# Top-32 attention and mixture of experts on one core: the threshold's selection moves from VectorE to GpSimd, and the pipeline gets a step longer

## Chip, cores and metric

One core of one Trainium2 chip runs the whole program. The metric is the device time of one execution in microseconds, the median of several runs.

## What is computed

Attention over 8 batches of 8 heads, 576 positions and 64 dimensions, in which each row keeps only its 32 largest scores. Its output, 4608 rows of 512, goes through a mixture of 8 experts, of which each row uses one.

```python
scores = scale * np.matmul(q, k.transpose(0, 1, 3, 2))
kth = np.partition(scores, -top_k, axis=-1)[..., -top_k:-top_k + 1]
scores = np.where(scores >= kth, scores, -1000000000.0)
attn = np.exp(scores - np.max(scores, axis=-1, keepdims=True))
attn = attn / (np.sum(attn, axis=-1, keepdims=True) + 1e-09)
x = np.matmul(attn, v)                        # -> rows of 512
logits = x @ w_gate + modality_bias[modality_id]
e_idx = np.argmax(logits, axis=1)
h = np.maximum(x[mask] @ w1[e], 0.0)          # mask: the rows of expert e
out[mask] = gate_w[mask, None] * (h @ w2[e])
```

## The kernel before

The scores are made in 288 tiles of 128 rows by 576, nine for each pair of heads, four pairs for each of the 8 batches. The main loop has one step `i` for each tile, and in a step each engine works on tiles of different age. In step `i`:

- TensorE makes the scores of tile `i + 2` (`qk`) and transposes the weights of tile `i - TL` (`trans`). It also makes parts of attention times v (`av`), transposes of later k and q (`prep`), transposes of finished rows (`xrow`, one row block of `x` each) and pieces of expert work.
- ScalarE copies scores out (`sevac`), makes a sign mask `K` (`sign`), which says which scores lie below the 24th largest and whose sum `n` tells how many do, exponentials (`expo`), and copies for TensorE.
- VectorE takes the 8 largest of seven parts of tile `i` (`subs`, L337), merges those of tile `i - 1` to its 24 largest (`chain`, L348 to L350), and takes the next 8 below them from the product `y` of an older tile (`find`, L379). When `find` has been made for three tiles, `pick` (L386 to L388) chooses among the nine values from the 24th to the 32nd the one that is the threshold: `eq` compares `i9s` with `n`, `jk` multiplies by the values, and an add over nine gives `kth`. In the same step the masked product `keep` (L399) of the oldest of these three tiles follows: scores at or above `kth`, times the exponentials.
- GpSimd runs `gate` (L403, one element, which waits for the `keep` of the step before), `pool_y` (L375, the product `y` of scores and sign mask), `below` (L362) and `small` (L356), in that order, and in some steps `fill` (L302), copies of tokens, and the issue of indirect DMAs: scatters of rows of `x` (L534) and of finished output rows (L724), each with a memset (L460) behind it.

VectorE's instructions of a step are put in order by `weave`: `chain` between `subs`, with `find` at place 2 and the operations on rows of `x` that `xrow` has left (`late`) at the places in `LOP`. What stands in the list `c_` comes after these: small operations of routing and of the expert schedule, `pick`, and `keep` last. Each engine runs its instructions in the order in which they are written.

Expert work is cut into slots of 256 rows of one expert. While the loop runs, a planner adds pieces of a slot to TensorE's queue: in each step it gets the budget `STEP` less the estimated `COST` of the attention work. 12 slots are handled in this woven way, with the weights in full fp32 (L685, L697, L709). The slots that remain go through a tail of their own (`slot`, L1074 and L1090), in which weights and rows are split in two parts each (`parts`, L1029, L1030), and three products are made of them. The first tail slot needs its weights split and its rows transposed (`turn_rows`, L1045). 19 slots are worked on in all, 7 of them in the tail.

```python
LT = LY + 1
LR = LT + 2
LE = LR - 1
TL = LR + 2
```

`LT` is the age of the tile of `find`, `LR` that of `keep`, `LE` that of `expo`, and `TL` that of `trans`. `RX` lists the steps of a batch's 36 in which `xrow` is made; the step after each has the operation on VectorE. `PJ` lists the steps of nine in which the transposes of the next pair's last rows, k and q are made. `AV3` and `AV7` cut `av` in parts for successive steps.

Of the kernel before, what the change touches and what calls it, by code (L numbers as in the profile page):

```python
# [9 lines left out]
FT = mybir.dt.float32  # L10
# [4 lines left out]
OP = mybir.AluOpType  # L15
# [6 lines left out]
CAP = 2.6  # L22
ME = 23
NB = 4
# [4 lines left out]
NW = 3  # L29
STEP = 3.3  # L30
STEPS = {"small": 0.1, "late": 0.5, "more": 0.15}
LJ = (5, 6)
PJ = (0, 1, 3)
VJ = 7
# [3 lines left out]
LY = KL + 2  # L38
LT = LY + 1
LR = LT + 2  # L40
LE = LR - 1
TL = LR + 2
YB = 3
XB = 3
RL = (5, 6)
RX = (1, 3, 10, 12, 14)
HG = 2
CUT = (12, 26)
PB = (2, 4)
AV3 = (0, 3, 5)  # L50
AV7 = (0, 2, 5)
COST = {"trans": 0.5, "qk": 0.5, "mix": 1.12, "rest": 0.22, "t": 0.11, "prep": 0.43, "logits": 1.2, "xrow": 0.54, "av": 0.49, "av8": 0.17}
# [17 lines left out]
def kernel(  # L70
# [301 lines left out]
    def pool_y(i):  # L372
        t = T[i]
        t["y"] = wk.tile([128, S], FT, name="y", bufs=YB)
        G.tensor_tensor(t["y"], t["S"], t["K"], op=OP.mult)  # L375
# [5 lines left out]
    def pick(i):  # L381

        t = T[i]
        eq, v = (wk.tile([128, 3, 9], FT, name=nm, bufs=1) for nm in ("eq", "jk"))
        n = t["n"][:, 0, :]
        return [lambda: V.tensor_tensor(eq, i9s, n[:, :, None].to_broadcast([128, 3, 9]), op=OP.is_equal),  # L386
                lambda: V.tensor_tensor(v, eq, t["mg"][:, :, 23:32], op=OP.mult),
                lambda: V.tensor_reduce(kth[:, i - 2:i + 1], v, axis=AX.X, op=OP.add)]  # L388

# [11 lines left out]
    def gate(i):  # L401

        G.tensor_scalar(spare[:, 0:1], T[i]["P"][0:1, 0:1], 1.0, 1.0, op0=OP.mult, op1=OP.mult)  # L403
# [442 lines left out]
    for i in range(LAST):  # L846
# [39 lines left out]
        for f in lp:  # L886
            f()
        cost += COST["rest"] * (len(lp) > 0)
        if p + 1 < NPAIR and j in PREP:
            prep(p + 1, PREP[j])  # L890
            cost += COST["t" if PREP[j] == "t" else "prep"]
# [27 lines left out]
        u = i - (TL + 1)  # L919
        if avs:  # L920
            c, f = avs.popleft()
            f()
            cost += c
        if ok(u) and u % 9 in (3, 7, 8):
# [29 lines left out]
        if ok(i - LT):  # L954
            b_.insert(2, lambda: find(i - LT))
            if (i - LT) % 3 == 2:
                c_ += pick(i - LT)
        for x, f in enumerate(lo):
# [24 lines left out]

        if ok(i - 1 - LR):
            gate(i - 1 - LR)
        if ok(i - LY):
            pool_y(i - LY)
        if ok(i - 1):
# [263 lines left out]
```

## Time and profile before

| what | us |
|---|---|
| median of 3 runs (1341.92 to 1348.37) | 1348.02 |
| the profiled execution | 1345.19 |
| span of its profile | 1343.4 |
| TensorE (PE) busy, share of the span | 1227.5, 91% |
| VectorE (DVE) | 1174.4, 87% |
| ScalarE (ACT) | 1001.1, 75% |
| GpSimd (POOL) | 630.0, 47% |

The profile is of one execution. Its times count from the first instruction; the execution's own time is 1.8 us longer than the span. Busy time is what the instructions of an engine cover. Matmuls are pipelined, and their ends are modelled, so a full TensorE in the profile need not be a TensorE at its peak. In the rows further down PE, DVE, ACT, POOL and SP are TensorE, VectorE, ScalarE, GpSimd and SyncE, and L399 is line 399.

### The profile page before, as it was taken

How to read it: one execution, taken by the hardware profiler on the slowest of the kernel's cores; microseconds unless marked ns; L12 is line 12 of the kernel's file. 1: busy time of each engine (PE TensorE's matmuls, PEld its weight loads, DVE VectorE, ACT ScalarE, POOL GpSimd, SP SyncE). 2: the span in 40 equal slices, each digit the busy share in tenths (PEclk: the TensorE clock that was granted, in tenths of full speed). 3: DMA queues.
4: the chain of work that ended last, by engine and by line, in shares of the span. 5: the costliest groups of instructions: out<-in, count | busy, mean ns of one | idle time of the engine just before them, and what ended most of it. 6: DMA issues, size and time to landing. Idle time of an engine off the chain costs nothing. (4 is left out here: it accounts for less than half of the span.)

```text
span 1343.4 us, 28995 instructions
## 1 busy us (share of the span) xinstructions
PE 1227.5 (91%) x8101; PEld 927.1 (69%) x8101; DVE 1174.4 (87%) x5958; ACT 1001.1 (75%) x1997; POOL 630.0 (47%) x1250
## 2 busy tenths in 40 slices
PE   6788887799998999999789999999999998999996
PEld 4666666576775867686567676876777665689985
DVE  3999999999999999999999999999999952666762
ACT  3788877888888879898888878988898851545642
POOL 2455547445565547554744575557554722011110
PEclk7899999899999999999989999999999999999998
DMA  5565334575545755653477556746664325656640
GB/s 118 137 177 124 81 81 115 147 198 142 135 116 163 201 134 160 185 142 81 131 189 193 134 157 165 176 112 196 166 176 126 124 80 177 219 181 228 236 170 15
DMA packets 206787, 201.05 MB, mean 150 GB/s; under 512 B 106221, under 2 KB 153325, under 8 KB 206608
## 3 DMA queue, kind: packets, MB, share of 16 engines
q1 hardware_dynamic: 200400, 179.48, 50.3%
q0 software_dynamic: 6208, 19.54, 4.0%
q8 instruction: 69, 1.13, 0.4%
q14 instruction: 110, 0.90, 0.2%
HBM read 118.63 MB, written 24.23 MB: 106 GB/s over the span
## 5 line engine op out<-in xcount | busy, mean ns | idle before, releaser
L337 DVE MAX8 cand<-Ssb 128x8 f32<-128x82 f32 (+1 forms) x2016 | 415.9, 229 | 19.9 <-ACT Ssb L330 19.8
L375 POOL TENSOR_TENSOR y<-Ssb,K 128x576 f32<-128x576 f32 x288 | 367.2, 1275 | 3.1 <-ACT K L369 2.6
L324 PE MATMUL S<-ks,qs 128*128 128x288 f32 x1024 | 234.9, 352 | 61.4 <-ACT Ssb L330 44.6
L330 ACT ACTIVATE Ssb<-S 128x576 f32<-128x576 f32 x288 | 187.9, 653 | 109.8 <-PE S L324 75.5
L369 ACT ACTIVATE K<-Ssb,n 128x576 bf16<-128x576 f32 x288 | 226.3, 786 | 31.2 <-POOL y L375 30.8
L324 PEld LDWEIGHTS S<-ks,qs 128*128 128x128 f32 x1024 | 160.0, 194 | 118.2 <-ACT Ssb L330 64.9
L393 ACT ACTIVATE ex<-Ssb,sm 128x576 f32<-128x576 f32 x288 | 224.2, 779 | 0.0
L399 DVE SCALAR_TENSOR_TENSOR P<-Ssb,kth,ex 128x576 f32<-128x576 f32 x256 | 213.5, 834 | 10.7 <-ACT ex L393 0.5
L379 DVE MAX8 mg<-y 128x8 f32<-128x576 f32 x288 | 213.8, 742 | 2.5 <-POOL y L375 2.5
L697 PE MATMUL E<-xgT,w1b 128*128 128x256 f32 x768 | 191.0, 392 | 6.7 <-ACT hT L701 4.5
L422 ACT ACTIVATE PT<-T 128x640 f32<-128x640 f32 (+1 forms) x288 | 190.0, 660 | 7.4 <-PE T L414 7.3
L709 PE MATMUL E<-w2b,hT 128*128 128x512 f32 x384 | 184.9, 605 | 2.2 <-ACT ot L719 1.3
L414 PE MATMUL T<-idf,P 128*128 128x128 f32 x1152 | 172.5, 277 | 0.0
L697 PEld LDWEIGHTS E<-xgT,w1b 128*128 128x128 f32 x768 | 140.6, 192 | 39.3 <-ACT hT L701 8.1
L443 PE MATMUL X<-PT,vm 128*64 128x256 f32 (+1 forms) x1536 | 163.2, 341 | 3.0 <-ACT st L260 2.5
L362 POOL TENSOR_SCALAR n<-mg 128x1 f32<-128x1 f32 x288 | 69.2, 240 | 201.9 <-DVE mg L350 198.2
L403 POOL TENSOR_SCALAR spare<-P 1x1 f32<-1x1 f32 x256 | 47.8, 187 | 219.4 <-DVE mg L348 204.2
L414 PEld LDWEIGHTS T<-idf,P 128*128 128x128 f32 x1152 | 138.0, 142 | 2.8 <-ACT PT L422 0.9
L443 PEld LDWEIGHTS X<-PT,vm 128*64 128x64 f32 x1536 | 80.8, 138 | 56.6 <-issue 27.0
L709 PEld LDWEIGHTS E<-w2b,hT 128*128 128x128 f32 x384 | 66.0, 190 | 64.2 <-issue 57.3
L1096 POOL DMA_INDIRECT out_dram<-ot,tk x14 | 14.0, 1003 | 131.0 <-ACT ot L1095 131.0
L348 DVE MAX8 mg<-cand 128x8 f32<-128x56 f32 x288 | 61.5, 214 | 0.2
(208 smaller groups left out, 2213.8 us busy)
## 6 DMA issues: line engine op xcount, KB each, us to landing
w1b<-in_moe_w_dram SPq DMA_DIRECT2D x76, 512.0 KB, 4.6
w2b<-in_moe_w_dram SPq DMA_DIRECT2D x76, 512.0 KB, 5.6
ks<-st SPq DMA_DIRECT2D x64, 288.0 KB, 3.9
qs<-st SPq DMA_DIRECT2D x128, 144.0 KB, 4.1
ks<-st SPq DMA_DIRECT2D x62, 256.0 KB, 5.0
xg<-xs SPq DMA_DIRECT2D x19, 516.0 KB, 5.9
km<-in_k_dram SPq DMA_DIRECT2D x64, 128.0 KB, 5.0
qm<-in_q_dram SPq DMA_DIRECT2D x64, 128.0 KB, 2.9
```

Source lines behind the costliest of these rows:

```text
L324: PE.matmul(ps[:, hf, u - a:v - a], l, d["ks"][:, x, h, u + o:v + o], start=(n == 0), stop=(n == len(terms) - 1), skip_group_check=(j == 8))
L337: return [lambda s=s: V.max(c[:, s * 8:s * 8 + 8], T[i]["S"][:, bnd[s]:bnd[s + 1]]) for s in range(NSUB)]
L369: A.activation(t["K"], t["S"], AF.Sign, scale=2.0 ** -24 - 1.0, bias=t["n"][:, 1, i % 3:i % 3 + 1], accum_out=t["n"][:, 0, i % 3:i % 3 + 1])
L375: G.tensor_tensor(t["y"], t["S"], t["K"], op=OP.mult)
L379: V.max(t["mg"][:, i % 3, 24:32], t["y"])
L393: A.activation(t["ex"], t["S"], AF.Exp, bias=t["s"][:, i % 3:i % 3 + 1])
L399: V.scalar_tensor_tensor(t["P"], t["S"], kth[:, i:i + 1], t["ex"], op0=OP.is_ge, op1=OP.mult, accum_out=dn)
L414: PE.transpose(T[i]["pt"][:, x, :], (Pm if c == 4 else Pb[c % 2])[:, h * 512 + x * 128:h * 512 + x * 128 + 128], idf)
L422: A.activation(o, T[i]["pt"][:, :n], AF.Copy)
L443: PE.matmul(o.rearrange("p (a b) -> p a b", a=2) if j < 8 else o, l, r, start=(c == 0), stop=(c == 4))
L697: PE.matmul(ps[:, f % 2], w1b[:, c, f * 128:(f + 1) * 128], xgT[:, c, :], start=(c == 0), stop=(c == KC - 1))
L709: PE.matmul(o["py"], hT[:, f, t * 128:(t + 1) * 128], w2b[:, f, :], start=(f == 0), stop=(f == FC - 1))
```

## The change

`pick` no longer compares. GpSimd makes five small operations for it: the difference `d` of `i9s` and `n`, its square, the square cut off at 1 (0 where both are equal, 1 elsewhere), its product with the values, and the values less that product. What is left is the chosen value and eight zeros, and VectorE adds the nine. The call stands one step later than before, behind `gate` and `pool_y`, which are now written ahead of the step's `c_`. `LR` is `LT + 3`: `keep`, `expo` and `trans` work on tiles one step older, and there is one more buffer of scores and one less of `y`. The rest are numbers of the planner, the places of `xrow`, the steps of the k and q transposes, the cut of `av`, and the place in the step at which the parts of `av` are issued.

```diff
-ME = 23
+ME = 24
-STEP = 3.3
+STEP = 3.2
-PJ = (0, 1, 3)
+PJ = (1, 2, 3)
-LR = LT + 2
+LR = LT + 3
-YB = 3
+YB = 2
-RX = (1, 3, 10, 12, 14)
+RX = (1, 4, 10, 13, 14)
-AV7 = (0, 2, 5)
+AV7 = (0, 3, 5)
...
     def pick(i):
         t = T[i]
-        eq, v = (wk.tile([128, 3, 9], FT, name=nm, bufs=1) for nm in ("eq", "jk"))
-        n = t["n"][:, 0, :]
-        return [lambda: V.tensor_tensor(eq, i9s, n[:, :, None].to_broadcast([128, 3, 9]), op=OP.is_equal),
-                lambda: V.tensor_tensor(v, eq, t["mg"][:, :, 23:32], op=OP.mult),
-                lambda: V.tensor_reduce(kth[:, i - 2:i + 1], v, axis=AX.X, op=OP.add)]
+        d, w, v = (wk.tile([128, 3, 9], FT, name=nm, bufs=b) for nm, b in (("pd", 1), ("pw", 1), ("pv", 2)))
+        y = t["mg"][:, :, 23:32]
+        G.tensor_tensor(d, i9s, t["n"][:, 0, :][:, :, None].to_broadcast([128, 3, 9]), op=OP.subtract)
+        G.tensor_tensor(w, d, d, op=OP.mult)
+        G.tensor_scalar(d, w, 1.0, 0.0, op0=OP.min, op1=OP.max)
+        G.tensor_tensor(w, d, y, op=OP.mult)
+        G.tensor_tensor(v, y, w, op=OP.subtract)
+        return lambda: V.tensor_reduce(kth[:, i - 2:i + 1], v, axis=AX.X, op=OP.add)
...
         cost += COST["rest"] * (len(lp) > 0)
+        if avs:
+            c, f = avs.popleft()
+            f()
+            cost += c
         if p + 1 < NPAIR and j in PREP:
...
         u = i - (TL + 1)
-        if avs:
-            c, f = avs.popleft()
-            f()
-            cost += c
...
         if ok(i - LT):
             b_.insert(2, lambda: find(i - LT))
-            if (i - LT) % 3 == 2:
-                c_ += pick(i - LT)
+        u = i - 1 - LT
+        if ok(i - 1 - LR):
+            gate(i - 1 - LR)
+        if ok(i - LY):
+            pool_y(i - LY)
+        if ok(u) and u % 3 == 2:
+            c_.append(pick(u))
...
         for f in c_:
             f()
 
-        if ok(i - 1 - LR):
-            gate(i - 1 - LR)
-        if ok(i - LY):
-            pool_y(i - LY)
```

How it moves instructions shows at three places. Each row is an instruction as the engine gets it: line, operation, what it writes and reads, and the output's size; x at the end counts equal ones that follow each other. Behind the diff the lines of the changed kernel are up to five higher.

The first place is GpSimd's queue around a step that ends a group of three, in the first batch whose rows are scattered. Before:

```order
L356 TENSOR_SCALAR sm<-mg 128x3
L534 DMA xs<-x_155,dest 38912x516
L460 MEMSET spare 1x1
L403 TENSOR_SCALAR spare<-P_123 1x1
L375 TENSOR_TENSOR y<-Ssb,K 128x576
L362 TENSOR_SCALAR n<-mg 128x1
```

Now:

```order
L407 TENSOR_SCALAR spare<-P_122 1x1
L375 TENSOR_TENSOR y<-Ssb,K 128x576
L387 TENSOR_TENSOR pd<-i9s,n 128x27
L388 TENSOR_TENSOR pw<-pd 128x27
L389 TENSOR_SCALAR pd<-pw 128x27
L390 TENSOR_TENSOR pw<-pd,mg 128x27
L391 TENSOR_TENSOR pv<-mg,pw 128x27
L538 DMA xs<-x_155,dest 38912x516
L464 MEMSET spare 1x1
L362 TENSOR_SCALAR n<-mg 128x1
```

The five operations stand right behind `y`, and the scatter has moved from ahead of the gate to behind them.

The second place is VectorE's queue at the end of such a step in the middle of the loop. Before:

```order
L350 MAX mg<-cand_9176 128x8
L337 MAX cand<-Ssb 128x8 x2
L386 TENSOR_TENSOR eq<-i9s,n 128x27
L387 TENSOR_TENSOR jk<-eq,mg 128x27
L388 TENSOR_REDUCE kth<-jk 128x3
L399 SCALAR_TENSOR_TENSOR P_123,den_129<-Ssb,kth,ex 128x576
```

Now:

```order
L337 MAX cand<-Ssb 128x8 x2
L350 MAX mg<-cand_9403 128x8
L337 MAX cand<-Ssb 128x8 x2
L392 TENSOR_REDUCE kth<-pv 128x3
L403 SCALAR_TENSOR_TENSOR P_123,den_129<-Ssb,kth,ex 128x576
```

`eq` and `jk` are gone, and the add reads `pv`, the last of GpSimd's five.

The third place is TensorE's queue from the last transposes of attention (of `xT`) to the first matmul of the tail. Before:

```order
L476 MATMUL X<-idf,xT 64x128 x4
L709 MATMUL E<-w2b,hT 128x512 x6
L685 MATMUL E<-idf,xg 128x128 x8
L697 MATMUL E<-xgT,w1b 128x256 x32
L709 MATMUL E<-w2b,hT 128x512 x10
L1045 MATMUL X<-idf,xg 128x128 x8
L709 MATMUL E<-w2b,hT 128x512 x6
L1074 MATMUL X<-xgh,w1h 128x256
```

Now:

```order
L480 MATMUL X<-idf,xT 64x128 x4
L713 MATMUL E<-w2b,hT 128x512 x11
L1050 MATMUL X<-idf,xg 128x128 x8
L1079 MATMUL X<-xgh,w1h 128x256
L1079 MATMUL X<-xgl,w1h 128x256
```

The twelfth woven slot (its transposes, 32 matmuls of the first layer and 16 of the second) is gone; 11 output matmuls of the eleventh slot are left where 6 were. An fp32 matmul of this list is two records in the trace.

## Rows read from the trace of the kernel before

**Rows 1.** Busy time by stage: stretch, its length, busy us (instructions) of each engine.

```profile
60.00:160.00 100.00, 85.59 (x696) 64.37 (x694) 97.98 (x531) 88.23 (x177) 53.05 (x107) 1.00 0.55 139
280.00:1065.00 785.00, 755.50 (x4959) 554.02 (x4957) 765.92 (x4111) 662.65 (x1363) 448.92 (x874) 0.99 0.59 156
940.00:1040.00 100.00, 100.00 (x668) 74.59 (x667) 97.45 (x529) 85.78 (x178) 52.97 (x109) 1.00 0.60 158
1065.00:1121.00 56.00, 51.88 (x318) 33.47 (x316) 36.53 (x151) 26.59 (x53) 20.91 (x43) 1.00 0.29 91
```

**Rows 2.** Timeline of VectorE, one pick step: start, duration, engine, line, operation.

```profile
551.69 0.16 DVE L386 TENSOR_TENSOR eq<-i9s,n 128x27 f32<-128x27 f32 x1
...
552.11 0.18 DVE L388 TENSOR_REDUCE kth<-jk 128x3 f32<-128x27 f32 x1
552.43 0.82 DVE L399 SCALAR_TENSOR_TENSOR P<-Ssb,kth,ex 128x576 f32<-128x576 f32 x1
```

**Rows 3.** Timeline of GpSimd, the same step.

```profile
549.66 1.27 POOL L375 TENSOR_TENSOR y<-Ssb,K 128x576 f32<-128x576 f32 x1
```

**Rows 4.** Single lines of GpSimd: durations in ns, min/median/max, first and last start.

```profile
L302 POOL TENSOR_SCALAR qbd<-qs x64: 233/244/929, 29.0 to 1060.9; 128x64 fp32r<-128x64 f32 x64
...
L356 POOL TENSOR_SCALAR sm<-mg x96: 184/199/248, 32.8 to 1083.3; 128x3 f32<-128x3 f32 x96
...
L460 POOL MEMSET spare<- x78: 88/89/91, 214.8 to 1333.5; 1x1 f32 x78
```

**Rows 5.** Timeline of GpSimd, a step with a scatter.

```profile
1045.06 1.06 POOL L534 DMA_INDIRECT xs<-x,dest  x1 [0.27 <-DVE cand L337]
...
1046.46 1.28 POOL L375 TENSOR_TENSOR y<-Ssb,K 128x576 f32<-128x576 f32 x1
1047.82 0.58 POOL L362 TENSOR_SCALAR n<-mg 128x1 f32<-128x1 f32 x1
```

**Rows 6.** Timelines of GpSimd and of VectorE, where `find` waits for `y`.

```profile
514.14 1.26 POOL L375 TENSOR_TENSOR y<-Ssb,K 128x576 f32<-128x576 f32 x1
...
515.43 0.76 DVE L379 MAX8 mg<-y 128x8 f32<-128x576 f32 x1 [0.70 <-POOL y L375]
```

**Rows 7.** Timeline of VectorE, a step with a row of x.

```profile
591.09 0.68 DVE L477 TENSOR_TENSOR x<-X,rd 128x512 f32<-128x512 f32 x1
591.68 0.21 DVE L349 MAX8 mg<-cand 128x8 f32<-128x56 f32 x1
```

**Rows 8.** Two lines of VectorE: durations in ns; then their groups: busy us, mean ns.

```profile
L386 DVE TENSOR_TENSOR eq<-i9s,n x96: 157/171/1121, 39.4 to 1089.7; 128x27 f32<-128x27 f32 x96
...
L399 DVE SCALAR_TENSOR_TENSOR P<-Ssb,kth,ex x256: 718/812/1803, 40.1 to 1091.2; 128x576 f32<-128x576 f32 x128
...
L386 DVE TENSOR_TENSOR eq<-i9s,n 128x27 f32<-128x27 f32 x96 | 22.5, 234 | 0.0
...
L399 DVE SCALAR_TENSOR_TENSOR P<-Ssb,kth,ex 128x576 f32<-128x576 f32 x256 | 213.5, 834 | 10.7 <-ACT ex L393 0.5 <-ACT st L260 0.5
```

**Rows 9.** Timeline of TensorE from slot 11's last output matmuls to the tail.

```profile
1115.07 5.32 PE L709 MATMUL E<-w2b,hT 128*128 128x512 f32 x12
1121.16 0.66 PE L685 MATMUL E<-idf,xg 128*128 128x128 f32 x4 [0.78 <-ACT ot L719]
...
1153.10 1.04 PE L1045 MATMUL X<-idf,xg 128*128 128x128 f32 x8
...
1158.72 0.68 PE L1074 MATMUL X<-xgh,w1h 128*128 128x256 f32 x1
```

**Rows 10.** Timeline of GpSimd in the tail: the second output issue of two slots.

```profile
1234.95 0.98 POOL L1096 DMA_INDIRECT out_dram<-ot,tk  x1 [5.15 <-ACT ot L1095]
...
1258.30 0.98 POOL L1096 DMA_INDIRECT out_dram<-ot,tk  x1 [5.15 <-ACT ot L1095]
```

**Rows 11.** Timeline of VectorE: the split of the first tail slot's rows, two halves.

```profile
1154.36 1.29 DVE L1030 TENSOR_TENSOR xgl<-X,xgh 128x512 fp32r<-128x512 f32 x2 [0.94 <-ACT xgh L1029]
```

**Rows 12.** DMA issues on the page: issues, KB each, median us to landing.

```profile
w2b<-in_moe_w_dram SPq DMA_DIRECT2D x76, 512.0 KB, 5.6
```

## The prediction

> **What bounds the kernel now.** I read the views from the coarse to the fine. Busy time by stage comes first [rows 1]: in 60:160 VectorE is 97.98 us busy of 100 with TensorE at 85.59, and in 940:1040 VectorE has 97.45 while TensorE shows 100.00. TensorE's share follows the expert work woven in; VectorE is full in both, so VectorE paces the attention loop, and TensorE has little room from 280 on (755.50 of 785). From 1065 to 1121 it turns round: TensorE 51.88 of 56, VectorE 36.53. There TensorE is the bound.
>
> The second view is the timeline of one step that ends a group of three (a pick step). VectorE finishes its maxima and starts `eq` at 551.69, `jk` (L387) follows, the add (L388) starts at 552.11 and the masked product (L399) at 552.43 [rows 2]. So the two operations that leave VectorE hold it for 552.11 - 551.69 = 0.42 us, 96 times. GpSimd, in the same step, ends the product `y` at 549.66 + 1.27 = 550.93 [rows 3].
>
> The third view is TensorE at the end: slot 12, the last of the woven kind, starts at 1121.16, when everything else of attention is done, and the first matmul of the split kind is at 1158.72 [rows 9]. So slot 12 hides under nothing and costs 37.6 us. A tail slot costs the distance of two output issues, 1258.30 - 1234.95 = 23.35 us [rows 10].
>
> **The change part by part.**
>
> *VectorE loses two operations.* 96 x 0.42 = 40.3 us less to issue. This is all on the path, if nothing takes the place.
>
> *GpSimd gets a chain of five in its place.* The order shows it behind `y` in the same step, each link waiting for the one before, and VectorE's add waiting for the last. That is the new wait; behind it on VectorE stand the masked product and the whole next step. The trace has no GpSimd operation of 27 elements. From below, the bound is the smallest operation of the queue, the memset with 0.09 us; from above it is a small one plus 27 elements at the pace of `y`, 0.199 + 27 x 1.274/576 = 0.26 [rows 3, 4]. Between them lie 0.199 for 3 elements and 0.244 for 64 [rows 4]. I take 0.20, the row nearest in kind; 64 elements add only 0.045 to it, so 27 should add little. A GpSimd operation that has had to wait for a semaphore starts about 0.08 after the end of its forerunner (1047.82 against 1046.46 + 1.28 = 1047.74) [rows 5]. From GpSimd's end to VectorE's start there is 0.03 (515.43 against 514.14 + 1.26 = 515.40) [rows 6]. So the add can start at 550.93 + 4 x 0.28 + 0.20 + 0.03 = 552.28. It is 0.59 later than VectorE could (551.69), and 0.17 later than it starts now (552.11).
>
> How much of this is covered is a matter of the neighbours, which I counted in the order of the changed kernel. Of the 96 pick steps, 54 have nothing extra ahead of the add: 54 x 0.17 = +9.2 us. In 13 stands one small operation of about 0.2 (such as `eq`): ready at 551.89, now 552.31, then 552.28, so 13 x -0.03 = -0.4. In 26 stands a row of x, which holds VectorE for 591.68 - 591.09 = 0.59 [rows 7]: it covers the chain, and these keep the whole gain, 26 x -0.42 = -10.9. Of the 35 rows of x inside the loop 14 fall into pick steps now, 26 after. Three steps have more: -1.3. Sum: **-3.4 us**, far from -40.3.
>
> The Trainium skill has a rule against this move: GPSIMD Engine Reference, section 4.1, gives elementwise work with two inputs to VectorE, since GpSimd is about twice as slow there. By it an operation would take twice the 0.17 us that `eq` takes on VectorE, some 0.35 (an estimate from that page), the chain 2.07, and the time would come near 1407; no row of this trace shows a small GpSimd operation as slow as that.
>
> *Order on GpSimd.* The scatter issues and the copies of tokens move behind `y`; now they stand ahead of it and make it late. A late `y` shuts out VectorE's operations with two inputs: `eq` lasts up to 1121 ns against a median of 171, the masked product 1803 against 812 [rows 8]. What this costs is the excess of all over the median: `eq` 22.5 us against 96 x 0.171 = 16.4, the product 213.5 against 256 x 0.812 = 207.9 [rows 8]. So 11.7 us at most come back. But a late chain now hits VectorE at once, while a late `y` had a step of slack. In 18 pick steps the order has an issue of an indirect DMA behind the `y` of the step before (1.06 us [rows 5]); 6 of them are output issues at the very end of the step, about 1 us late each, and 12 are scatters that mostly fit: up to +10. I take **-2**, with -11.7 and +10 as ends.
>
> *One slot moves from the woven kind to the tail.* The lower budget (3.2 for 3.3) makes the planner start slot 11 about three tiles later, and the loop ends before slot 12 begins: the order has 11 woven slots and then the tail. Every row that is worked on stays. Away goes 37.6; a tail slot comes in, +23.3. After the last scores TensorE has three matmul groups of slot 10 and eight transposes of slot 11 more than now: 3 x 5.32/6 = 2.7 and 2 x 0.66 = 1.3 [rows 9], +4.0. The transposes of the next slot's rows (1.04, now under slot 12 [rows 9]) stand bare between the last output matmul and the tail, with the split behind them, of which the first half must be through before the matmuls can run on (1.29/2 = 0.65 on VectorE, about as much on ScalarE ahead of it [rows 11]): with the hand-overs about +3. Sum **-7.3 us**. Its weight loads and the five last scatters have the eleven output matmuls (11 x 0.89 = 9.8 us) and the first tail slot as their cover; without it one load would add its 5.6 us [rows 12].
>
> *Edits that I cost at nothing.* The masked product one step later and one buffer more of the scores: one product more to drain, 0.81 us [rows 8], which lies under the TensorE work of 1065:1121. Two buffers of `y` for three: the next `y` waits for the last masked product anyway. The k and q transposes and the parts of attention times v: VectorE's pace covers their order on TensorE; k's copies to the stacked tile leave SP's queue one step later and still have three steps until they are read. If TensorE were the pace here, their order could cost a few tenths a pair.
>
> Sum: -3.4 - 2 - 7.3 = -12.7. Against the profiled execution's 1345.2 us that is 1332.5; the median of the runs stands 2.8 above that execution, so I expect **1335 us**.
>
> **The rivals.**
>
> *A: the chain is short enough* (forecast; operations of 0.17 to 0.225 us). Each 0.01 us of an operation is 0.05 in a chain and, over the 93 steps that feel it, 4.6 us.
>
> *B: the chain is nearly hidden.* With 0.09 per operation the add could start at 551.73; then 54 x -0.38, 13 x -0.42, 26 x -0.42 and -1.3 make -38. TensorE has only 29.5 us to spare in 280:1065 [rows 1], so I count about -24 of it: 1345.2 - 24 - 2 - 7.3 + 2.8 = 1315. Against it: no GpSimd operation with an input is under 0.18 us [rows 4].
>
> *C: TensorE takes over the pace.* Whatever VectorE saves is lost to a TensorE that is full from 280 on; only the slot is left: 1348.0 - 7.3 = 1341. For it: 100.00 in 940:1040. Against it: VectorE is as full there as where TensorE is at 85.59.
>
> *D: GpSimd becomes the bound of every pick step, and the kernel gets slower.* With 0.26 per operation the chain is 1.62 and the add starts at 552.58, 0.47 later than now: 54 x 0.47 + 13 x 0.27 - 26 x 0.12 - 1.3 = +24.5, less 9.3 is +15: 1363. It decides from 0.227 us per operation on, where the gain of the slot is used up, and is beyond what a measurement tells from no change (0.5%, 6.7 us) from 0.242 on. For it: the row of 64 elements stands at 0.244, and no small one has two inputs. Against it: elements add little [rows 4]. The rule of the page above is the far end of this rival, with 0.03 of its chance.
>
> *E: nothing to measure* (operations of 0.225 to 0.242, or late chains that eat the slot's gain): 1347 to 1354.
>
> That the change doesn't do what it says is out for the slot and the five operations: both are in the order.
>
> **How the numbers follow.** A 0.50, B 0.10, C 0.07, D 0.22, E 0.11. A's own range is 1322 to 1347; of it 0.42 is below 1341.3, which with B makes faster by over 0.5% 0.52. The rest of A (0.08), C and E make 0.26 for no change, D is 0.22. The range 1316 to 1360 leaves out half of B and the upper half of D, about 0.16.
>
> **What would show it.** Right: VectorE's add waits for GpSimd in the 54 bare pick steps (some 0.6 us each, 30 us or more in all in the table of waits) and hardly in those with a row of x; the chain takes about 1.3 us; `y` is never late behind a scatter; 11 woven slots, and eight tail slots 23.3 us apart. Wrong: links of more than 0.3 us (D) or under 0.2 (B); a loop no shorter though the add does not wait (C); a gap of more than 5 us between slot 11 and the tail (the loads have lost their cover).

## The result, and the profile after

The changed kernel takes 1365.62 us (median of 4 runs, 1364.41 to 1365.80); the kernel before, run beside it, 1348.19. The ratio is 1.0137, with a 95% interval of 1.0106 to 1.0169: slower by 1.4%, against a forecast of 1335 with 1360 as its upper end. The profiled execution took 1365.55, its span is 1363.8.

Cut at the first and the last candidate maxima (L337) and at the last masked product on VectorE, and at the first matmul of the tail on TensorE, the two spans compare so (us):

| stage | before | after | difference |
|---|---|---|---|
| to the first maxima | 20.3 | 20.2 | -0.1 |
| the loop over 288 tiles | 1057.7 | 1076.0 | +18.3 |
| drain, to the last masked product | 16.6 | 19.7 | +3.1 |
| to the first tail matmul | 64.1 | 36.1 | -28.0 |
| tail (7 slots before, 8 after) | 184.7 | 211.8 | +27.1 |

The forecast had the loop at -5.4 and the rest at -7.3; it came to +18.3 and +2.1. First the busy time by stage, of the changed kernel, columns as in [rows 1]:

```profile
60.00:160.00 100.00, 85.36 (x675) 64.09 (x675) 92.28 (x497) 85.17 (x172) 67.21 (x152) 0.98 0.52 130
940.00:1040.00 100.00, 92.83 (x611) 68.49 (x610) 90.42 (x492) 81.25 (x168) 65.93 (x153) 0.97 0.59 154
280.00:1065.00 785.00, 739.48 (x4858) 545.26 (x4858) 725.24 (x3892) 650.07 (x1338) 525.16 (x1190) 0.98 0.58 151
```

Against [rows 1] VectorE fell from 97.98 to 92.28 and from 97.45 to 90.42, and TensorE from 100.00 to 92.83 in the late stretch. GpSimd rose from 53 to 67. No engine is full any more: something waits. Which wait it is stands in the groups of instructions of the changed kernel (busy us, mean ns | idle before them, and what ended it):

```profile
L387 POOL TENSOR_TENSOR pd<-i9s,n 128x27 f32<-128x27 f32 x96 | 21.7, 226 | 0.0
L388 POOL TENSOR_TENSOR pw<-pd 128x27 f32<-128x27 f32 x96 | 22.3, 232 | 7.5
L389 POOL TENSOR_SCALAR pd<-pw 128x27 f32<-128x27 f32 x96 | 20.2, 211 | 8.4
L390 POOL TENSOR_TENSOR pw<-pd,mg 128x27 f32<-128x27 f32 x96 | 22.9, 238 | 8.0
L391 POOL TENSOR_TENSOR pv<-mg,pw 128x27 f32<-128x27 f32 x96 | 23.2, 241 | 7.5
L392 DVE TENSOR_REDUCE kth<-pv 128x3 f32<-128x27 f32 x96 | 17.3, 180 | 64.0 <-POOL pv L391 63.6
L403 DVE SCALAR_TENSOR_TENSOR P<-Ssb,kth,ex 128x576 f32<-128x576 f32 x256 | 209.3, 818 | 9.1 <-ACT PT L426 0.4
```

VectorE's add waits 63.6 us for the last link, where `eq` and `jk` held VectorE for 40.3 before. The masked product (818 ns against 834 in [rows 8]) hardly changed. A pick step with nothing extra ahead of the add shows the chain; the timeline of VectorE first, then GpSimd's, which answer to [rows 2] and [rows 3]:

```profile
563.83 0.38 DVE L337 MAX8 cand<-Ssb 128x8 f32<-128x82 f32 x2
564.84 0.18 DVE L392 TENSOR_REDUCE kth<-pv 128x3 f32<-128x27 f32 x1 [0.63 <-POOL pv L391]
565.16 0.82 DVE L403 SCALAR_TENSOR_TENSOR P<-Ssb,kth,ex 128x576 f32<-128x576 f32 x1
```

```profile
562.09 1.27 POOL L375 TENSOR_TENSOR y<-Ssb,K 128x576 f32<-128x576 f32 x1
563.33 0.23 POOL L387 TENSOR_TENSOR pd<-i9s,n 128x27 f32<-128x27 f32 x1
563.63 0.23 POOL L388 TENSOR_TENSOR pw<-pd 128x27 f32<-128x27 f32 x1
563.95 0.21 POOL L389 TENSOR_SCALAR pd<-pw 128x27 f32<-128x27 f32 x1
564.25 0.24 POOL L390 TENSOR_TENSOR pw<-pd,mg 128x27 f32<-128x27 f32 x1
564.57 0.24 POOL L391 TENSOR_TENSOR pv<-mg,pw 128x27 f32<-128x27 f32 x1
```

From the end of `y` (562.09 + 1.27 = 563.36) to the start of the add (564.84) it is 1.48 us, where the prediction had 1.35. The mean link is 0.23 long, and links start 0.30 to 0.32 apart. The add waited 0.63.

Three other kinds of pick step cost what the prediction did not see. The first is a step whose `y` is late; GpSimd, then VectorE:

```profile
395.76 1.60 POOL L538 DMA_INDIRECT xs<-x,dest  x1 [0.17 <-issue]
...
398.11 1.27 POOL L375 TENSOR_TENSOR y<-Ssb,K 128x576 f32<-128x576 f32 x1
...
400.58 0.24 POOL L391 TENSOR_TENSOR pv<-mg,pw 128x27 f32<-128x27 f32 x1
```

```profile
400.85 0.18 DVE L392 TENSOR_REDUCE kth<-pv 128x3 f32<-128x27 f32 x1 [2.01 <-POOL pv L391]
```

The scatter issue of the step before holds GpSimd for 1.60; `y` ends about 1.4 us later than usual, the chain with it, and the add waits 2.01. The second kind has a small operation of the routing behind the add (VectorE):

```profile
353.41 0.17 DVE L544 TENSOR_TENSOR r_l<-lgb,bias_all 128x40 f32<-128x40 f32 x1
354.11 0.18 DVE L392 TENSOR_REDUCE kth<-pv 128x3 f32<-128x27 f32 x1 [0.53 <-POOL pv L391]
354.21 0.19 DVE L545 TENSOR_REDUCE r_mx<-r_l 128x5 f32<-128x40 f32 x1
354.43 0.20 DVE L546 TENSOR_TENSOR r_z<-r_l,r_mx 128x40 f32<-128x40 f32 x1
354.55 0.81 DVE L403 SCALAR_TENSOR_TENSOR P<-Ssb,kth,ex 128x576 f32<-128x576 f32 x1
```

VectorE stands idle 0.53 with L545 ready (it reads what L544 made at 353.41) and L546 queued behind the add. The third is a step with a row of x, in which the chain is not quite covered either: the add starts at 607.41, right behind maxima of 606.99, but 3.07 us into the step, as in a bare one:

```profile
606.99 0.37 DVE L337 MAX8 cand<-Ssb 128x8 f32<-128x82 f32 x2
607.41 0.18 DVE L392 TENSOR_REDUCE kth<-pv 128x3 f32<-128x27 f32 x1
```

### The profile page after: what moved, and what is told of

It is laid out like the page before. It is cut to its first block, busy times and chain, and to the rows that moved or that the text cites. A ratio compares the mean times of both kernels' runs of the same rounds, so it can differ in the third digit from the quotient of the medians.

```text
span 1363.8 us, 29424 instructions
## 1 busy us (share of the span) xinstructions
PE 1229.7 (90%) x8155; PEld 936.4 (69%) x8155; DVE 1155.4 (85%) x5795; ACT 1009.2 (74%) x2009; POOL 760.1 (56%) x1730
## 5 line engine op out<-in xcount | busy, mean ns | idle before, releaser
L337 DVE MAX8 cand<-Ssb 128x8 f32<-128x82 f32 (+1 forms) x2016 | 416.3, 230 | 19.1 <-ACT Ssb L330 19.0
L324 PE MATMUL S<-ks,qs 128*128 128x288 f32 x1024 | 240.1, 358 | 84.7 <-ACT Ssb L330 44.5
L324 PEld LDWEIGHTS S<-ks,qs 128*128 128x128 f32 x1024 | 163.0, 197 | 147.8 <-ACT Ssb L330 64.8
L403 DVE SCALAR_TENSOR_TENSOR P<-Ssb,kth,ex 128x576 f32<-128x576 f32 x256 | 209.3, 818 | 9.1 <-ACT PT L426 0.4
L701 PE MATMUL E<-xgT,w1b 128*128 128x256 f32 x704 | 176.8, 393 | 2.5 <-ACT hT L705 1.2
L713 PE MATMUL E<-w2b,hT 128*128 128x512 f32 x352 | 171.0, 605 | 1.0 <-ACT ot L723 0.8
L701 PEld LDWEIGHTS E<-xgT,w1b 128*128 128x128 f32 x704 | 129.2, 194 | 31.1 <-issue 7.3
L362 POOL TENSOR_SCALAR n<-mg 128x1 f32<-128x1 f32 x288 | 63.5, 221 | 140.2 <-DVE mg L350 129.6
L713 PEld LDWEIGHTS E<-w2b,hT 128*128 128x128 f32 x352 | 59.7, 190 | 53.8 <-issue 47.7
L392 DVE TENSOR_REDUCE kth<-pv 128x3 f32<-128x27 f32 x96 | 17.3, 180 | 64.0 <-POOL pv L391 63.6
```

Source lines behind the costliest of these rows:

```text
L324: PE.matmul(ps[:, hf, u - a:v - a], l, d["ks"][:, x, h, u + o:v + o], start=(n == 0), stop=(n == len(terms) - 1), skip_group_check=(j == 8))
L337: return [lambda s=s: V.max(c[:, s * 8:s * 8 + 8], T[i]["S"][:, bnd[s]:bnd[s + 1]]) for s in range(NSUB)]
L403: V.scalar_tensor_tensor(t["P"], t["S"], kth[:, i:i + 1], t["ex"], op0=OP.is_ge, op1=OP.mult, accum_out=dn)
L701: PE.matmul(ps[:, f % 2], w1b[:, c, f * 128:(f + 1) * 128], xgT[:, c, :], start=(c == 0), stop=(c == KC - 1))
L713: PE.matmul(o["py"], hT[:, f, t * 128:(t + 1) * 128], w2b[:, f, :], start=(f == 0), stop=(f == FC - 1))
```

## The experiments

All times are medians; each run stood beside runs of the kernel before, whose median lay between 1343.4 and 1345.2 in five groups of runs. Single executions of that kernel lie between 1338.5 and 1350.0, and the interval of a ratio is 2 to 6 us to either side, so a difference of a few us between two runs is not exact to its first digit.

**Run 1: the picks back on VectorE, all else as changed.** `pick` gives `eq`, `jk` and the add to VectorE again:

```diff
-            c_.append(pick(u))
+            c_ += pick(u)
```

> The changed kernel, but the thresholds are picked on VectorE again (comparison, product and add, one step later than before); order on GpSimd, slots and everything else stay as changed. Theory 1 (the loss in the loop is VectorE waiting for GpSimd's chain: 63.6 us of waits in place of 40.3 us of work): the wait of the add for GpSimd is gone, the loop shortens by 15 to 25 us, 1341 to 1350 us in all. Theory 2 (the other shifts, later masked product, transposes, attention times v, cost the loop its time and the wait only stands where another one would): 1358 us or more.

1343.59 us, ratio 1.000 (0.998 to 1.002). Theory 1 held: the loop went from 1076.0 to 1050.2. The move of two operations to GpSimd alone costs 22.0 us at this budget (at 3.3 it is 4.5, runs 10 and 14). Since only the picks differ, the two traces can be set beside each other step by step, from the end of one masked product to the end of the next (287 steps, us, changed kernel less run 1):

| step | count | sum | mean |
|---|---|---|---|
| pick, nothing extra, `y` on time | 34 | +11.6 | +0.34 |
| pick, nothing extra, `y` over 0.06 late | 16 | +16.9 | +1.06 |
| pick with small operations | 19 | +9.9 | +0.52 |
| pick with a row of x | 26 | -5.8 | -0.22 |
| all others | 192 | -6.6 | -0.03 |

In the changed kernel `y` is late in 26 pick steps (25 of them in the table: 16 bare, 3 with small operations, 6 with a row of x), and 18 of those have an issue of an indirect DMA between the `y` before and this one. TensorE's clock is not the cause: 24.7 of the 26.0 us lie in the 260 steps in which both traces show the upper of its two levels (2.4 GHz) throughout.

**Run 2: the kernel before with 11 woven slots.**

```diff
-ME = 23
+ME = 8
```

> The kernel before, with nothing changed but that the planner starts no new slot in the last tiles: 11 woven slots and 8 in the tail, as in the changed kernel. Prediction's term for this: -7.3 us, so 1341 us. Rival (the tail's first two slots lose the cover of their loads and splits, as the changed kernel shows with 29.3 and 26.1 us for them in place of 23.3): -1 to +4 us, 1347 to 1352 us.

1338.93, ratio 0.9958 (0.9940 to 0.9976): -5.8 us. That it lies near -7.3 is luck: the -7.3 includes the +4.0 of TensorE work that the lower budget leaves behind, and this run has the budget of 3.3. Its own term is -37.6 + 23.3 + 3 = -11.3, and half of that came. The loop is the same to 0.3 us at every 24th tile; what follows it went from 265.4 to 259.1. In it the tail grew from 184.7 to 211.7, by 27.0 for one slot more, where the prediction had 23.3. The rival's time did not come, but its mechanism shows: the tail's first two slots take 27.7 and 29.2 us here, 25.0 and 28.0 in the kernel before. The tail of the changed kernel (211.8) is no longer than this one.

**Run 3: the chain at the end of the step of `find`, the add one step later.**

```diff
-            c_.append(pick(u))
+            c_.append(adds.pop())
...
         if ok(i - 1):
             below(i - 1)
+        if ok(i - LT) and (i - LT) % 3 == 2:
+            adds.append(pick(i - LT))
```

> The changed kernel, but GpSimd's five operations stand at the end of the step whose maxima they read, behind the scaling of the threshold candidate, and VectorE adds the nine values in the next step as now. Theory 1 (the add waits for a chain that is issued too late): its waits for GpSimd fall from 63.6 to under 15 us, and the time falls by 35 to 60 us, to 1305 to 1330 us, where TensorE begins to limit. Theory 2 (the wait only stands in the place of another): the time stays within 10 us, 1355 to 1370. A third outcome, 1335 to 1355, would say that the chain, now under the masked product, delays the product or the next y by locks.

1339.79, ratio 0.9972 (0.9954 to 0.9989): the add waits 0.7 us in all, yet only 25.8 us of the 35 to 60 came, the third outcome. The chain now runs beside the masked product, and both are longer in the groups of run 3:

```profile
L403 DVE SCALAR_TENSOR_TENSOR P<-Ssb,kth,ex 128x576 f32<-128x576 f32 x256 | 221.7, 866 | 9.1 <-ACT Ssb L330 0.4
L390 POOL TENSOR_TENSOR pw<-pd,mg 128x27 f32<-128x27 f32 x96 | 42.3, 441 | 8.0
```

The product has 12.4 us more than in the changed kernel, and a link of 27 elements went from 238 to 441 ns in the mean (its median stayed at 238, the longest took 840).

**Run 4: the chain ahead of `y`.** Two statements exchanged:

```diff
-        if ok(i - LY):
-            pool_y(i - LY)
         if ok(u) and u % 3 == 2:
             c_.append(pick(u))
+        if ok(i - LY):
+            pool_y(i - LY)
```

> The changed kernel with one pair of calls exchanged: GpSimd's five operations ahead of y in the step, not behind it. Theory 1: the chain ends some 1.85 us into the step, before VectorE is ready for the add (2.3), so the add stops waiting; y ends about 1.5 us later in every third step and now the masked product or the next maxima meet it: waits of 64 us go, some 20 to 40 come, 1330 to 1350 us. Theory 2: no change, 1360 to 1370.

1352.78, ratio 1.0078 (1.0052 to 1.0104). The add waits 10.8 us instead of 63.6, as Theory 1 said, but the later `y` lies beside the masked product, whose L403 group grew from 209.3 to 230.7 us; the time ended 3 us above the range.

**Run 5: small operations ahead of the add.**

```diff
-            c_.insert(2 * x, f)
+            c_.insert(x, f)
```

> The changed kernel, but the small operations of a step that stood behind the add now stand ahead of it on VectorE. Theory 1 (where small operations are issued behind the waiting add they cannot fill the wait; 15 pick steps lose 0.3 to 0.6 us so): -4 to -8 us, 1357 to 1362 us. Rival (these steps are limited elsewhere): within 2 us of the changed kernel.

1364.18, ratio 1.0134 (1.0108 to 1.0160): Theory 1 missed, and the time lies in the rival's range (1.4 us below the changed kernel). Its reason does not fit, though: the 19 steps with small operations gained 3.8 us, and the others gave it back, so that the loop is 2.0 us longer in the profiled execution.

**Run 6: seven links.**

```diff
         G.tensor_tensor(w, d, d, op=OP.mult)
+        G.tensor_tensor(d, w, w, op=OP.mult)
+        G.tensor_tensor(w, d, d, op=OP.mult)
         G.tensor_scalar(d, w, 1.0, 0.0, op0=OP.min, op1=OP.max)
```

> The changed kernel with two more links in GpSimd's chain (the square is squared twice more, which changes no result). Theory 1 (every link is 0.31 us of path in each pick step that waits): the add of a bare step goes from 3.07 to 3.69 us into the step; 96 x 0.62 = 60 us at most, 45 to 58 us in all, 1410 to 1424 us. Theory 2 (the chain's wait only replaces others): under 20 us, below 1386.

1417.03, ratio 1.0530 (1.0503 to 1.0557): 51.4 us for two links, 0.54 per pick step, inside Theory 1's range. The group of the add in run 6:

```profile
L394 DVE TENSOR_REDUCE kth<-pv 128x3 f32<-128x27 f32 x96 | 17.4, 181 | 118.8 <-POOL pv L393 118.4
```

The wait grew by 118.4 - 63.6 = 54.8 us. Added links go to the path almost whole: 51.4 of at most 60 us.

**Run 7: three links.**

```diff
-        G.tensor_tensor(w, d, d, op=OP.mult)
-        G.tensor_scalar(d, w, 1.0, 0.0, op0=OP.min, op1=OP.max)
-        G.tensor_tensor(w, d, y, op=OP.mult)
-        G.tensor_tensor(v, y, w, op=OP.subtract)
+        G.tensor_scalar(w, d, 0.0, 1.0, op0=OP.is_equal, op1=OP.mult)
+        G.tensor_tensor(v, y, w, op=OP.mult)
```

> The changed kernel with two links fewer: difference, a comparison with zero (one input), product with y; the same thresholds. Theory 1: the add of a bare step goes from 3.07 to about 2.45 us into the step, hardly behind the 2.34 at which VectorE is ready; -0.62 in the bare steps and 0 to -0.3 in the others: 30 to 45 us less, 1321 to 1336 us, unless TensorE limits first as it seems to with the chain a step ahead (1339.8): then 1336 to 1342. Theory 2: above 1350.

1337.46, ratio 0.9937 (0.9912 to 0.9961): -28.2 us, just short of Theory 1's 30 to 45 and inside the range that it named for a limit by TensorE, which this run does not show. Groups of run 7:

```profile
L388 POOL TENSOR_SCALAR pw<-pd 128x27 f32<-128x27 f32 x96 | 34.2, 356 | 8.4
...
L390 DVE TENSOR_REDUCE kth<-pv 128x3 f32<-128x27 f32 x96 | 17.0, 177 | 29.8 <-POOL pv L389 27.5
```

The comparison takes 356 ns where the minimum took 211, so the way from the end of `y` to the add is 0.49 shorter (0.99 for 1.48), not 0.62; about two thirds of the waits that are left stand in the steps with a late `y`.

**Run 8: three of the five links one step earlier.** The difference, square and minimum, which need only the counts, go behind `y` of the step before:

```diff
             c_.append(pick(u))
+        if ok(i - LT) and (i - LT) % 3 == 2:
+            mask(i - LT)
```

> The changed kernel, but the three links that need only the counts (difference, square, minimum) stand behind y one step earlier; behind y of the pick step stay two. Theory 1: the add finds its values ready at 2.25 us into the step, so it waits only behind late y; and unlike with the whole chain a step ahead (1339.8) nothing of GpSimd's chain runs beside the masked product, whose lengthening cost 12 us there: 1326 to 1338 us. Rival (TensorE is the pace then): 1338 to 1343.

1343.42, ratio 1.000 (0.998 to 1.002): a miss of Theory 1, and of the rival by 0.4 us only. The early links push back what follows them on GpSimd: in the bare pick steps `y` ends 2.25 us into the step in the mean, against 1.88 in the changed kernel. Of these 50 steps 32 are shorter than in run 1, most of them by 0.44 us, and 18 are longer, by up to 1.75.

**Run 9: the kernel before with 11 slots, and on GpSimd the gate and `y` ahead of scatters and copies.**

```diff
+        if ok(i - 1 - LR):
+            gate(i - 1 - LR)
+        if ok(i - LY):
+            pool_y(i - LY)
         for x, f in enumerate(lo):
...
-        if ok(i - 1 - LR):
-            gate(i - 1 - LR)
-        if ok(i - LY):
-            pool_y(i - LY)
```

> The kernel before with two things of the change alone: 11 woven slots, and on GpSimd the gate and y ahead of the scatter issues and the copies of tokens in each step. The run with 11 slots alone stands at 1338.9. My prediction's term for the order is -2 (ends -11.7 and +10): 1337. Theory 1 (the 7.5 us that the loop of the changed kernel gains with its picks back on VectorE come from this order): 1331 to 1334. Rival (they come from the masked product one step later or the shifted transposes): 1337 to 1341.

1329.19, ratio 0.9878 (0.9832 to 0.9924): the best of all runs, 9.7 us below run 2. Its groups answer to [rows 8]:

```profile
L386 DVE TENSOR_TENSOR eq<-i9s,n 128x27 f32<-128x27 f32 x96 | 18.9, 197 | 0.0
...
L399 DVE SCALAR_TENSOR_TENSOR P<-Ssb,kth,ex 128x576 f32<-128x576 f32 x256 | 209.3, 818 | 11.6 <-ACT ex L393 1.2 <-DVE kth L388 0.5
```

`eq` fell from 22.5 to 18.9 and the product from 213.5 to 209.3: 7.8 us, which covers the 6.5 by which the loop is shorter than in run 2. Most of the rest of the 9.7 lies in the tail (209.3 against 211.7), on which the order has no bearing; tails of eight slots took 209.3 to 213.0 us in all these profiles.

**Run 10: the changed kernel with the budget of 3.3 and 11 slots.**

```diff
-ME = 24
+ME = 8
-STEP = 3.2
+STEP = 3.3
```

> The changed kernel with the budget of TensorE at 3.3 again and no new slot begun in the last tiles: 11 woven slots, each begun as early as before, so that slot 11 stands 6 tiles ahead of the last scores and not behind them. Theory (the end of the changed kernel is 8.5 us longer than that of the kernel before with 11 slots because the lower budget leaves that much TensorE work behind the last tile): -5 to -9 us, 1356 to 1361. Rival (the loop pays for what the end gains, TensorE being near full): within 2 us of 1365.

1357.53, ratio 1.0095 (1.0066 to 1.0124): -8.1 us, as the theory had it. The loop stayed (1075.3); what follows it fell by 7.8. TensorE's expert matmuls (tile E) from the start of the last masked product to the tail, in the changed kernel, run 2 and run 10 (stretch, length, TensorE busy and instructions of that tile):

```profile
1115.80:1151.97 36.17, 19.97 (x53) 1.00 0.36 119
```

```profile
1094.60:1125.49 30.89, 15.26 (x32) 0.97 0.37 118
```

```profile
1114.30:1145.40 31.10, 14.14 (x30) 1.00 0.30 102
```

The lower budget leaves 4.7 us more of them there than run 2 has.

**Run 11: the chain behind `y` in the step of `find`, the add in the next step.** As run 3, but right after the maxima are issued:

```diff
         weave(a_, b_)
+        if ok(i - LT) and (i - LT) % 3 == 2:
+            adds.append(pick(i - LT))
         for f in c_:
```

> The changed kernel with all five links, issued behind y in the step in which VectorE finds the last maxima that they read, so before the masked product of that step ends; VectorE adds in the next step as now. Theory (three things made the loss: the chain behind y, late y, and small operations behind the waiting add; all three go when the chain has a step of slack, and it runs mostly ahead of the masked product): the add waits under 5 us in all, the masked product is lengthened by under 6 us; the loop comes 10 to 30 us below that with picks on VectorE (1343.6): 1314 to 1334. Rival (VectorE's freed 0.42 us per pick step is taken by TensorE's pace): 1336 to 1344.

1343.15, ratio 0.9992 (0.9970 to 1.0015): the theory missed, and the time lies in the rival's range. The add waits 0.7 us, as the theory said, and most bare pick steps are 0.44 us shorter than run 1's (18.8 us for the 50), but the 192 steps without an add are 26.7 longer. Groups of run 11:

```profile
L403 DVE SCALAR_TENSOR_TENSOR P<-Ssb,kth,ex 128x576 f32<-128x576 f32 x256 | 224.0, 875 | 9.9 <-ACT ex L397 0.8 <-ACT Ssb L330 0.4
L390 POOL TENSOR_TENSOR pw<-pd,mg 128x27 f32<-128x27 f32 x96 | 45.5, 474 | 8.1 <-POOL pd L389 0.2
```

The product has 14.7 us more than in the changed kernel, where the theory allowed 6, and the find now waits 12.1 for `y`. So the rival's reason, TensorE's pace, is not what these rows show.

**Run 12: the same with three links, budget 3.3 and 11 slots** (the edits of runs 7, 10 and 11 together).

> As the run with the chain behind the find, with three links (difference, comparison with zero, product) and the budget of 3.3 with 11 slots. Theory: 4 to 10 us below that run. Rival (TensorE's pace): no better than 3 us below it.

1341.79, ratio 0.9974 (0.9950 to 0.9997): 1.4 below run 11, as the rival's number had it.

**Runs 13 and 14: three links, and the picks on VectorE, both with the budget of 3.3 and 11 slots** (runs 7 and 1 with the edit of run 10).

> The changed kernel with three links on GpSimd and with the budget of 3.3 and 11 slots. If the terms add: 1337.5 (three links) less 8.1 (what the budget gave the changed kernel) is 1329.4, as good as the order alone (1329.2). Rival (with the late y of 17 pick steps and TensorE fuller in the loop, what VectorE saves is lost): 1333 to 1338.

> The changed kernel with the picks on VectorE and with the budget of 3.3 and 11 slots: everything of the change but the move to GpSimd and the lower budget. If the terms add: 1343.6 - 8.1 = 1335.5, 6 us behind the run with three links. Rival (the later masked product, the shifted transposes and rows of x cost nothing beside the order): 1329, as the order alone; then what three links save on VectorE is worth nothing either.

1344.94 (ratio 1.0007, 0.9988 to 1.0026) and 1353.03 (1.0077, 1.0047 to 1.0106): both outside all their ranges, and the step from the budget of 3.2 wrong in sign. What the higher budget gave run 10 it takes from these. So the terms do not add, and run 14 stands 24 us behind run 9, though both have the picks on VectorE, the new order, 11 slots and the budget of 3.3.

**Runs 15 to 17: which of the other shifts that is.** Run 14 with the k and q transposes as before; with all of TensorE's order as before; with only the parts of attention times v and the rows of x as before (`PJ` in the first two, `RX`, `AV7` and the place of the waiting parts of `av` in the last two):

```diff
-PJ = (1, 2, 3)
+PJ = (0, 1, 3)
-RX = (1, 4, 10, 13, 14)
+RX = (1, 3, 10, 12, 14)
-AV7 = (0, 3, 5)
+AV7 = (0, 2, 5)
```

> The run with picks on VectorE, budget 3.3 and 11 slots (1353.0), with the transposes of t, k and q in the steps of the kernel before (0, 1, 3). Theory 1 (k one step later makes the loads of the stacked tile late, and the scores with them: 15.9 us of waits of the scores for that DMA against 7.8 in the run with the order alone): -10 to -20 us, 1333 to 1343. Rival (the shifted parts of attention times v or the later masked product cost it): within 4 us.

> The same run with all of the transposes, the parts of attention times v and the rows of x as before; of the change stay the order on GpSimd, the masked product one step later and 11 slots. Theory (the shifts on TensorE cost 24 us at the budget of 3.3, the later product nothing): 1327 to 1333, as the order alone (1329.2). Rival (the later masked product, with one buffer of scores more and one of y less, costs it): 1345 to 1355.

> The same run with only the parts of attention times v and the rows of x as before; the transposes of k and q stay shifted. Theory 1 (k and q): within 4 us of 1353. Rival: 1333 to 1343.

1361.62 (ratio 1.0136, 1.0097 to 1.0175), 1348.89 (1.0018, 1.0002 to 1.0033) and 1345.47 (1.0000, 0.9985 to 1.0016). Theory 1 and the rival of the first and the theory of the second fell; the rival of the second held, and that of the third came nearest (2.5 us above its range). Undoing the shift of k and q alone even costs 8.6 us. Run 16 differs from run 9 in the masked product alone, which comes one step later (with the pick a step later, one buffer of scores more and one of `y` less): 19.7 us. The waits of run 9, then of run 16 (engine, line, waited for: us, times, longest):

```profile
POOL y L375 <- ACT K L369: 12.1, 16, 1.9
DVE x L477 <- PE X L476: 8.5, 5, 3.2
```

```profile
POOL y L375 <- ACT K L369: 28.6, 33, 3.3
DVE x L477 <- PE X L476: 16.3, 16, 2.8
PE X L443 <- DVE cand L337: 10.7, 6, 3.3
```

The product's transposes and attention times v follow it one step later. By these waits signs then come later for `y`, the products of rows of x later for VectorE, and attention times v itself waits 10.7 us behind VectorE's candidates. Set beside run 9 tile by tile, run 16 has 2.5 us more before its first masked product (the pipeline is one step deeper) and 14.9 us more from the first to the last. 12.2 of these lie in steps in which TensorE's clock is at its upper level (2.4 GHz) in both traces. And 9.9 lie in two of a batch's 36 steps, those in which VectorE takes the third and the fourth row of x: there it stands idle for TensorE's transposes (L476) 8.4 us in all, against 0.1 in run 9. The longest of these waits in run 16 and the same row in run 9, TensorE first, then VectorE; run 9:

```profile
754.36 0.60 PE L476 MATMUL X<-idf,xT 128*128 128x128 f32 x4
```

```profile
756.63 0.67 DVE L477 TENSOR_TENSOR x<-X,rd 128x512 f32<-128x512 f32 x1
```

Run 16:

```profile
764.86 2.74 PE L709 MATMUL E<-w2b,hT 128*128 128x512 f32 x6
...
768.74 0.60 PE L476 MATMUL X<-idf,xT 128*128 128x128 f32 x4
```

```profile
769.38 0.69 DVE L477 TENSOR_TENSOR x<-X,rd 128x512 f32<-128x512 f32 x1 [2.84 <-PE X L476]
```

In run 9 the row's transposes stand ahead of the step's output matmuls; in run 16 they come a step later, behind six of these. The buffer of `y` that goes costs no wait that the trace shows: in run 16 `y` waits for signs alone.

```profile
L375 POOL TENSOR_TENSOR y<-Ssb,K 128x576 f32<-128x576 f32 x288 | 367.0, 1274 | 28.8 <-ACT K L369 28.6
```

The other 5.0 us between the masked products are not traced to a cause, and 3.5 of the 22.2 by which the profiled executions differ lie in the tail, whose code is the same in both. Shifting k and q as well takes 3.4 of the 19.7 back (run 17).

**Run 18: three links with TensorE's order as before** (run 13 with the edits of run 16).

> Three links on GpSimd, budget 3.3, 11 slots, and all of TensorE's order as before. If what three links save on VectorE (6.1 us at the budget of 3.2, 8.1 at 3.3) is still there with the end and TensorE's order at their best: 1321 to 1325, below the order alone (1329.2). Rival (TensorE's pace, or the late y): 1328 to 1336.

1344.49, ratio 1.0004 (0.9990 to 1.0018): the expected gain did not come, and the time lies above the rival's range as well. It is 4.4 below run 16, which has the same later product and the picks on VectorE; beside run 9, which also picks on VectorE but has no later product, nothing is gained.

## Why the prediction was wrong

Put in one row, each from the runs above, the parts come to (us):

| part | predicted | measured | from |
|---|---|---|---|
| 12th woven slot to the tail | -11.3 | -5.8 | run 2 to the kernel before |
| order on GpSimd | -2 | -9.7 | run 9 to run 2 |
| masked product one step later | 0 | +19.7 | run 16 to run 9 |
| k, q, attention times v, rows of x shifted | 0 | +4.1 | run 14 to run 16 |
| budget 3.2 for 3.3 | +4.0 | -9.4 | run 1 to run 14 |
| picks on GpSimd | -3.4 | +22.0 | changed kernel to run 1 |
| all | -12.7 | +20.9 | changed kernel to 1344.7 (before, beside runs 1 to 4) |

The -11.3 and the +4.0 are the two parts of the prediction's -7.3. Beside its own runs of the kernel before (1348.19) the changed kernel is 17.4 behind, not 20.9. The rows hold in this order only. With the picks on GpSimd the same budget costs 8.1 (run 10), and at 3.3 the move of the picks costs 4.5 (run 10 to run 14). As I read it, though no run isolates it, a step that the chain lengthens also gives TensorE more time, and a lower budget then only leaves more for the end.

*Picks on GpSimd, the step that failed.* The chain and its cover were to give -3.4 and cost +22.0 (+4.5 at the budget of 3.3). "I take 0.20, the row nearest in kind" was too low: the five links have 0.226, 0.232, 0.211, 0.238 and 0.241, by rival D's formula +10.5 in place of -3.4 (mean 0.23: the add at 552.43, 0.15 later than in the forecast, in 93 steps). That is rival D's mechanism, at its threshold, but only about half of the way to +22. That rival D's 1363 lies near the result is chance: it has 0.26 us for a link and nothing for the later product. The rest are three other readings of the prediction. "12 are scatters that mostly fit" was wrong, and with it the sign "`y` is never late behind a scatter": 16 bare pick steps with a late `y` lost 1.06 each. The small operations, costed at -0.03 in each of 13 steps, stood partly behind the add: 19 steps at +0.52. The row of x was to keep the whole 0.42 and kept 0.22. Of the excess 6.6 came back in the other steps. The place was right: the add waits 0.6 us in bare steps, and 63.6 in all where "30 us or more" was named.

*Order on GpSimd, too small.* The end of -11.7 was nearly reached (-9.7, of which 6.5 lie in the loop). The argument that late chains would eat it was sound for the changed kernel, but belongs to the picks, where it was left out of the sum.

*Masked product one step later, costed at nothing, the second failure.* I looked at its own 0.81 us in the drain and not at what is fixed to it: everything that TensorE does with the product moves by one step against everything that follows the tile's number. Run 16 shows the price: 2.5 us for a pipeline one step deeper, and 14.9 in the steps, of which 9.9 in two that take a row of x, where VectorE waits for TensorE. The sentence "If TensorE were the pace here, their order could cost a few tenths a pair" was said of other edits, but it names the engine that is waited for there. With the picks on VectorE the lower budget mends the loop (1067.0 in run 14, 1050.2 in run 1) and pays at the end. With the picks on GpSimd it mends nothing (1075.3 in run 10, 1076.0 in the changed kernel).

*End.* Put at -7.3, it came to +2.1. The drain is 3.1 longer, where nothing was put in. The stretch to the first tail matmul fell by 28.0, where -37.6 + 4.0 + 3 = -30.6 was put in. And the tail grew by 27.1 for one slot of 23.3: its slots stand 23.34 us apart in the middle, as forecast, but its first ones are longer without slot 12 ahead of them (run 2). What the lower budget leaves of slot 11 was forecast about right: 4.0 us, against 4.7 more than in run 2.

*The rule against the move.* The Trainium skill (GPSIMD Engine Reference, section 4.1) speaks against giving such work to GpSimd. With five links in the pick step this case agrees. With three it does not: the picks on GpSimd then came 4.4 to 8.1 us below those on VectorE (runs 7, 13 and 18 against 1, 14 and 16). The factor of about two in the Trainium skill does not hold at this size: 0.226 to 0.241 us with two inputs on GpSimd against 0.171 of `eq` and 0.188 of `jk` on VectorE (medians) is 1.3. And "no row of this trace shows a small GpSimd operation as slow as that" overlooked single ones of 0.929 us (L302, [rows 4]) and 0.58 (L362, [rows 5]); runs 3 and 11 show where such times come from.

*Left open:* why the budget and the picks do not add is not shown, nor what makes up the 5.0 us of run 16's steps that are not in the two rows of x, and a GpSimd without late `y` was not tried with the chain.

## What to carry to other kernels

A helper engine's chain is priced by its latency behind its own queue, not by the time that it takes off the full engine: count links with their gaps, what in the queue can make the first one late, and what stands behind the wait. A chain moved out of the way can land beside an operation of the neighbour and lengthen it (here the masked product, by 12.4 and 14.7 us in runs 3 and 11). And "one step later" moves everything that hangs on the step, so price the phase, not the operation; the part of a change that seems a by-product (here the order on the queue) may be the one worth keeping.

## What the runs showed of the hardware beyond what I expected

A GpSimd operation of 27 elements takes about as long as one of 3 or 64 (0.199 and 0.244 us, [rows 4]), 0.21 to 0.24 us, and a link that depends on it starts 0.07 to 0.09 after its end. A comparison with zero on the same 27 elements takes 0.356 (run 7). Beside VectorE's masked product the same small operation takes up to 0.85 us, so that one link's mean went from 238 to 441 and 474 ns in runs 3 and 11, and the product grows from 818 to 866 and 875 ns in the mean. It holds for one input too: the scaling of three elements (L356), 199 ns in [rows 4], has a mean of 494 in the changed kernel, where it falls beside the product.
